# Strided attention in half-array blocks of three classes, with one exponential a pair

## The chip, the cores and the metric

The kernel runs on one core of one Trainium2 chip. A core has TensorE (PE; its weight loads are listed as PEld), VectorE (DVE), ScalarE (ACT), GpSimd (POOL) and SyncE (SP), which run side by side and wait for each other by semaphores. SP issues most transfers here, POOL the indirect ones. The metric is the time of one execution on the device, in microseconds (us); lower is better. Of the kernel before, nine runs are known: a median of 743.74 us, 740.93 to 749.4.

## The reference, cut to what matters

```python
# q, k, v: 8 batches, 8 heads, 576 positions, 64 wide, float32
rel = pos[:, None] - pos[None, :]
mask_local = (rel >= 0) & (rel < 32)                                  # heads 0 to 3
mask_strided = (rel >= 0) & (pos[None, :] % 32 == pos[:, None] % 32)  # heads 4 to 7
attn = softmax(where(mask, q @ k.T / 8, -1e9)); x = attn @ v          # then (8, 576, 512)
# a mixture of 8 experts over the 4608 rows of x
logits = x @ w_gate; local_gate = sigmoid(x @ w_local)
# row by row: the expert is argmax(logits) where local_gate < 0.5 (and at s == 0), else that of the row before
out[b, s] = softmax(logits[b, s])[e] * (relu(x[b, s] @ w1[e]) @ w2[e])
```

In the strided heads a position sees only those of its own class, pos % 32. There are 32 classes of 18 positions each, so the useful part of a 576 by 576 score matrix is 32 triangles of 18 by 18.

## The kernel before, in words

The program has two parts in one order written out by hand: `attention`, which also computes the gate logits and starts the routing, and `Experts.run`, the expert matmuls. The change lies in the first, except for the shape of one small array.

Attention goes over 32 pairs of heads, `order` = 8 batches times `PAIRS` = 4; in each batch pairs 0 and 1 are local, pairs 2 and 3 strided. A pair has two units, `g` = 0 and 1. The loop at line 414 runs over steps `n`; step `n` works on several pairs at once:

- `load(n + 4)`: q and k of the pair four ahead, by SP into one of five buffers `qk`; with the first local and the first strided pair of a batch also v (`vl`, `vs`). At `n` = 6 the weights of the first expert, 4 MB, follow in the same queue.
- `scores(n)` and `mask(n)`. Line 252 multiplies k by q in blocks. Head `h` of the pair lies on partitions 64h to 64h+63, so two heads use the upper and lower half of the array's rows. Each head has a PSUM bank of its own in the tile `sps` (two buffers). Line 256 takes the exponential on ACT into `e`. A local unit has three blocks of 96 queries by 128 keys for each head, masked afterwards by DVE (line 263). Strided units first have their mask put into PSUM by a bfloat16 matmul with the identity (line 246); no DVE mask follows.
- `store_x(n - 2)`: every second pair, the normalised rows go to DRAM (`xd`), by SP: two transfers for the local half of a batch, ten for the strided half (line 307).
- `turn_x(n - 2)`: line 317 transposes the rows of the pair into `tps`, the tile of the pool `psT`, which has one buffer; ACT copies it into `xT` (line 321).
- `values(n - 1)` and `norm(n - 1)`: line 276 multiplies `e` by v into `vps` (two buffers), in halves of 64 queries that go to the upper and the lower partitions; v has a column of ones, which gives the sums. DVE takes the reciprocal (289) and multiplies (290).
- `logits` of the batch whose last pair was turned in this step (`n - 2`, so `n` = 4b + 5): line 336, again into `psT`, then four copies into `lT`, in turn by ACT (339), DVE (340), ACT (342) and DVE (344), each waiting for the one before. `gates` a step later (`n - 3`): line 354 and some twelve small DVE instructions.
- From `n` = 19 on, for the first four batches, the router's steps: `turn`, `scan`, `hot`, `count`, `slot`, `back` (on PE, ACT, DVE), then 20 scatters on POOL (line 577), two placed in each step, and among them the gather of the first two tiles of rows for the experts (line 737) at `n` = 29.

The strided classes are in five groups: four of `GC` = 7 classes (126 positions) and one of 4 (72). A block of scores is 126 keys by 126 queries, with the classes interleaved, `position * 7 + class`. Unit 0 has groups 0 and 1 of both heads, unit 1 groups 2, 3 and 4. The mask, one bfloat16 tile `maskS`, is worked out at the start by POOL iotas and some 24 DVE instructions (lines 192 to 215), because the class of a row is a remainder by 7 or 4. In DVE's queue these stand before the first mask of the local pairs.

SP's transfers use eight completion semaphores in turn, so a transfer is issued only after the transfer eight places before it has landed.

Of the kernel before, what the change touches and what calls it, by code (L numbers as in the profile page):

```python
# [37 lines left out]
PL, GC, GT = S // STRIDE, 7, 5  # L38
GR = STRIDE - GC * (GT - 1)
GK, GL = PL * GC, PL * GR  # L40
# [102 lines left out]
def attention(ctx, tc, qkl, qks, vl, vs, wg, xd, ident, router, moe):  # L143
# [15 lines left out]
    def load(b, pair):  # L159
        local = pair < PAIRS // 2  # L160
        src = qkl if local else qks
        t = inp.tile([P, qkl.shape[-1]], F32, name="qk")
        st["qk", b, pair] = t
        nc.sync.dma_start(out=t[:, 0:src.shape[-1]], in_=src[b, pair % 2])
        if pair % 2 == 0:
            shape = [LK, LT, 4, V1] if local else [GK, GT, 4, V1]
            t = vals.tile(shape, F32, name="vl" if local else "vs")
            nc.sync.dma_start(out=t, in_=(vl if local else vs)[b])
            st["v", b, local] = t
# [22 lines left out]
    maskS = consts.tile([GK, 2 * GK + GL], BF16, name="maskS")  # L192
    for n, c in ((GK, GC), (GL, GR)):
        i = consts.tile([GK, n], I32, name=f"i{n}")
        cls = consts.tile([GK, n], F32, name=f"cls{n}")
        div = consts.tile([GK, n], F32, name=f"div{n}")
        both = []
        for mult, pattern in ((1, [[0, n]]), (0, [[1, n]])):

            nc.gpsimd.iota(i, pattern=pattern, base=0, channel_multiplier=mult)  # L200
            t = consts.tile([GK, n], F32, name=f"cls{n}{mult}")
            nc.vector.tensor_copy(t, i)
            nc.vector.tensor_scalar(i, i, 65536 // c + 1, None, Alu.mult)
            nc.vector.tensor_scalar(i, i, 16, None, Alu.arith_shift_right)
            nc.vector.tensor_copy(div, i)
            nc.vector.scalar_tensor_tensor(t, div, -float(c), t, Alu.mult, Alu.add)
            both.append(t)
        nc.vector.tensor_tensor(cls, both[0], both[1], op=Alu.not_equal)
        nc.vector.tensor_scalar(cls, cls, NEG, None, Alu.mult)
        nc.gpsimd.affine_select(out=cls, in_=cls, compare_op=Alu.is_ge, fill=NEG, base=0, pattern=[[1, n]],  # L210
                                channel_multiplier=-1)
        if n == GK:
            nc.vector.tensor_copy(maskS[:, 0:2 * n].rearrange("p (a x) -> p a x", a=2), across(cls, [n, 2, n]))
        else:
            nc.vector.tensor_copy(maskS[:, 2 * GK:], cls)
# [16 lines left out]
    def spans(u):  # L232

        if u.local:
            return [(3 * u.g + i, LQ, i * LQ) for i in range(3)]
        return [(j, GK if j < GT - 1 else GL, i * GK) for i, j in enumerate(range(2 * u.g, 2 + 3 * u.g))]

    def scores(u):
        t = st["qk", u.b, u.pair]
        kb, width = (LK, LQ) if u.local else (GK, GK)  # L240
        ps = psS.tile([P, 2, 512], F32, name="sps")
        sp = spans(u)
        n = sp[-1][2] + sp[-1][1]
        if not u.local:
            for h in range(2):
                nc.tensor.matmul(ps[0:GK, h, 0:n], lhsT=identb[0:GK, 0:GK],  # L246
                                 rhs=maskS[:, 0:n], start=True, stop=False, skip_group_check=True)
        for j, w, c in sp:
            m = kb if u.local else w
            for h in range(2):  # L250
                r = slice(h * DH, (h + 1) * DH)
                nc.tensor.matmul(ps[0:m, h, c:c + w], lhsT=t[r, S + j * width:S + j * width + m],  # L252
                                 rhs=t[r, j * width:j * width + w],
                                 start=(u.local and c == 0), stop=True, skip_group_check=True)
        e = work.tile([P, 2, 2 * GK + GL], F32, name="e")
        nc.scalar.activation(e[0:kb, :, 0:n], ps[0:kb, :, 0:n], Act.Exp, bias=0.0, scale=1.0 / DH ** 0.5)  # L256
# [9 lines left out]
    def values(u):  # L266

        vt = st["v", u.b, u.local]
        i2 = u.pair % 2
        ps = psV.tile([P, 2, 3, V1], F32, name="vps")  # L270
        for i, (j, w, c) in enumerate(spans(u)):
            m = LK if u.local else w
            for h in range(2):
                for a in range(2):
                    q0 = c + a * (w - HALF)
                    nc.tensor.matmul(ps[a * HALF:(a + 1) * HALF, h, i], lhsT=u.e[0:m, h, q0:q0 + HALF],  # L276
                                     rhs=vt[0:m, j, 2 * i2 + h], start=(i == 0 and h == 0), stop=True,
                                     skip_group_check=True)
        u.ps = ps

    def norm(u):
        i2 = u.pair % 2
        if i2 == 0 and u.g == 0:
            st["x", u.b, u.local] = rows.tile([P, LT if u.local else GT, D // 2], F32, name="xl" if u.local else "xs")
        xt = st["x", u.b, u.local]
        sp = spans(u)
        j0, n = sp[0][0], len(sp)
        rc = sums[:, u.n, :, 0:n]
        nc.vector.reciprocal(out=rc, in_=u.ps[:, :, 0:n, DH])
        nc.vector.tensor_tensor(xt[:, j0:j0 + n, i2 * P:(i2 + 1) * P].rearrange("p i (h d) -> p h i d", h=2),  # L290
                                u.ps[:, :, 0:n, 0:DH], spread(rc, [P, 2, n, DH]), op=Alu.mult)

    def store_x(u):
# [3 lines left out]
        for a in range(2):  # L297
# [5 lines left out]
            for j in range(GT):  # L303
                c = GC if j < GT - 1 else GR
                w = c * PL // 2
                o = dst.rearrange("(p c) d -> p c d", c=STRIDE)[a * PL // 2:(a + 1) * PL // 2, j * GC:j * GC + c]
                nc.sync.dma_start(out=o, in_=src[a * (P - w):a * (P - w) + w, j])

    def turn_x(b, pair):
# [5 lines left out]
        n = LT if local else GT  # L315
        for t in range(n):
            nc.tensor.transpose(ps[:, t], src[:, t], ident)  # L317
        o = st["xT", b][:, pair]

        def halves(o, i, w):  # L320
            nc.scalar.copy(out=o.rearrange("p (t a x) -> p t a x", a=2, x=w // 2),
                           in_=pick_halves(i, w))

        if local:
            halves(o, ps[:, 0:LT], LQ)
        else:
            halves(o[:, 0:4 * GK], ps[:, 0:GT - 1], GK)
            halves(o[:, 4 * GK:], ps[:, GT - 1:GT], GL)

    def logits(b):  # L330
        xT = st["xT", b]
        ps = psT.tile([P, 2, 512], F32, name="tps")
        n = GK * (GT - 1)
        for a, c in ((0, slice(0, n)), (1, slice(n, S))):
            for kk in range(DK):
# [4 lines left out]
        nc.vector.tensor_copy(lT[0:64, n:], ps[0:64, 1, 0:GL])  # L340
        o = lT[64:].rearrange("p (y c) -> p y c", c=STRIDE)
        nc.scalar.copy(out=o[:, :, 0:GC * (GT - 1)].rearrange("p y (j c) -> p j y c", c=GC),
                       in_=ps[64:, 0, 0:n].rearrange("p (j y c) -> p j y c", j=GT - 1, c=GC))
        nc.vector.tensor_copy(o[:, :, GC * (GT - 1):], ps[64:, 1, 0:GL].rearrange("p (y c) -> p y c", c=GR))
        st["lT", b] = lT

    def gates(b):

        ps = psV.tile([P, 2, 3, V1], F32, name="vps").rearrange("p a i e -> p (a i e)")
# [43 lines left out]
    for n, u in enumerate(u for both in units for u in both):  # L393
        u.n = n

    also = {n: [] for n in range(len(units) + 3)}
    also[2] = [router.constants]
    n = PAIRS * RB + 3
# [15 lines left out]
    for n in range(len(units) + 3):  # L414
# [10 lines left out]
        if 0 <= n - 2 < len(units) and n != len(units):  # L425
            turn_x(*order[n - 2])
# [6 lines left out]
        elif n == len(units) + 1:  # L433
            moe.turn(moe.first, spare, 0)
# [1034 lines left out]
```

## Time and profile before

The profiled execution took 745.11 us, 1.4 more than the median, and its span, from the first to the last instruction, is 743.3 us.

| | us |
|---|---|
| median of nine runs | 743.74 |
| profiled execution, its span | 745.11, 743.3 |
| PE busy, PEld busy | 693.7, 620.2 |
| DVE, ACT, POOL busy | 380.7, 198.9, 134.2 |
| attention part, up to the first expert matmul | 0 to 196.6 |
| one batch of attention, steps 4 to 7 | 24.33 to 43.08 |
| scatters of the router | 123 to 139, 170 to 180 |
| mean granted clock | 0.961 |

The page gives busy time by engine, then the span in 40 slices of 18.6 us, where a digit is the busy share in tenths. The timeline shows merged instructions: start in us, length in us, engine, line, operation, `out<-in`, shapes, the count, and in brackets the engine's idle time before it and what ended it. A length there reaches to the modelled end of the last matmul, which overlaps with what follows, so stretches of TensorE are best measured from start to start. A shape `64*126 64x126` is 64 rows by 126 columns of the array, and the 126 moving columns. A float32 matmul call appears as two records, each with a weight load of its own.

### The profile page before, as it was taken

To read this page: it belongs to the slowest core of one execution; us is meant where nothing else is said; L and a number is where in the kernel's file an instruction comes from. 1 tells how busy PE (TensorE), PEld (TensorE's weight loads), DVE (VectorE), ACT (ScalarE), POOL (GpSimd) and SP (SyncE) were. 2 spreads that over 40 slices of the span, in tenths; PEclk is the share of its full clock that TensorE was granted. 3 is DMA by queue.
4 is the path that set the end of the run, shared out by engine and by line. 5 is a ranking of instruction groups with operands and counts; after the bars stand their busy time and mean duration, and the time that the engine had idled before them with its cause. 6 is when DMAs were issued, how large, how long until landed. Compare 5 with 4: busy or idle time off the path is not lost.

```text
span 743.3 us, 15189 instructions
## 1 busy us (share of the span) xinstructions
PE 693.7 (93%) x6170; PEld 620.2 (83%) x6170; DVE 380.7 (51%) x896; ACT 198.9 (27%) x360; POOL 134.2 (18%) x150
## 2 busy tenths in 40 slices
PE   7999998597798799999999999999999999999993
PEld 5887887385697689899998899999999999889992
DVE  6567765372474534473563266466346646324341
ACT  2544442241321122222222222212222222212320
POOL 3000002305147221211121120131012112111001
PEclk9999999596899799999999999999999999999998
DMA  9798788732430023504322612520161342010100
GB/s 324 272 367 260 275 280 263 214 89 70 147 143 30 10 80 123 194 30 170 109 74 88 211 58 91 197 86 31 43 232 58 132 151 73 32 36 31 30 29 27
DMA packets 38057, 95.83 MB, mean 129 GB/s; under 512 B 5358, under 2 KB 14574, under 8 KB 37888
## 3 DMA queue, kind: packets, MB, share of 16 engines
q1 hardware_dynamic: 29616, 73.77, 29.1%
q0 software_dynamic: 7744, 20.08, 8.5%
q8 instruction: 64, 1.05, 0.6%
q14 instruction: 105, 0.86, 0.4%
q10 hardware_dynamic: 528, 0.07, 0.1%
HBM read 74.93 MB, written 20.02 MB: 128 GB/s over the span
## 4 chain that ended last, share of the span: by engine, by line
PE 88%; DVE 3%; issue 3%; another core or an unknown queue 2%; DMA 1%; ACT 1%; POOL 1%; POOLq 0%; DVEq 0%
PE lps L807 32%; PE mps L843 31%; PE sps L252 6%; PE vps L276 6%; PE tps L317 3%; PE xps L750 2%; PE lps L898 2%; PE mps L909 2%; PE sps L246 2%; PE vps L354 1%; PE tps L336 1%; DMA qk<-in_qks_dram 1%; DMA x<-xd,gi 1%; DVE xl L290 1%
## 5 line engine op out<-in xcount | busy, mean ns | idle before, releaser
L807 PE MATMUL lps<-tt,ws 128*128 128x128 f32 x912 | 108.8, 275 | 1.9 <-issue 1.8
L807 PEld LDWEIGHTS lps<-tt,ws 128*128 128x128 f32 x912 | 105.3, 192 | 2.2 <-issue 2.2
L763 POOL DMA_INDIRECT out_dram<-y,tab x40 | 45.8, 1146 | 332.8 <-DVE y L795 274.2
L843 PE MATMUL mps<-wt,k 128*128 128x256 f32 x456 | 101.6, 379 | 0.0
L843 PEld LDWEIGHTS mps<-wt,k 128*128 128x128 f32 x456 | 86.6, 190 | 11.8
L795 DVE TENSOR_TENSOR h<-lps,u 128x512 f32<-128x512 f32 x57 | 39.4, 691 | 80.7 <-PE lps L807 68.1
L807 PE MATMUL lps<-xt,w1t 128*128 128x128 f32 x608 | 76.0, 279 | 0.0
L807 PEld LDWEIGHTS lps<-xt,w1t 128*128 128x128 f32 x608 | 74.2, 196 | 1.9 <-issue 1.0
L843 PE MATMUL mps<-w2t,h 128*128 128x256 f32 x304 | 72.7, 382 | 0.0
L577 POOL DMA_INDIRECT slots<-tok,idx x40 | 41.0, 1024 | 145.2 <-DVE tok L568 133.2
L843 PEld LDWEIGHTS mps<-w2t,h 128*128 128x128 f32 x304 | 57.0, 193 | 7.1
L252 PE MATMUL sps<-qk 64*128 64x96 f32 (+2 forms) x704 | 54.8, 285 | 5.8 <-issue 4.6
L737 POOL DMA_INDIRECT x<-xd,gi x40 | 39.5, 986 | 112.8 <-PE lps L807 33.2
L794 ACT ACTIVATE h<-h 128x512 f32<-128x512 f32 x57 | 35.9, 630 | 88.6 <-DVE h L795 85.4
L252 PEld LDWEIGHTS sps<-qk 64*128 64x128 f32 (+2 forms) x704 | 45.1, 186 | 15.8 <-issue 13.3
L256 ACT ACTIVATE e<-sps 128x576 f32<-128x576 f32 (+1 forms) x64 | 41.4, 651 | 57.7 <-PE sps L252 39.8
L807 PE MATMUL lps<-xt,ws 128*128 128x128 f32 x304 | 39.0, 284 | 6.1 <-DVE h L795 6.1
L807 PEld LDWEIGHTS lps<-xt,ws 128*128 128x128 f32 x304 | 37.1, 199 | 6.3 <-DVE h L795 6.3
L795 DVE TENSOR_TENSOR u<-lps,p 128x512 f32<-128x512 f32 x19 | 13.1, 692 | 55.7 <-PE lps L807 51.8
L794 ACT ACTIVATE h<-lps 128x512 f32<-128x512 f32 x23 | 13.7, 597 | 97.8 <-PE lps L807 71.5
L807 PE MATMUL lps<-tt,w1t 128*128 128x128 f32 x304 | 37.9, 276 | 1.5 <-issue 1.1
L807 PEld LDWEIGHTS lps<-tt,w1t 128*128 128x128 f32 x304 | 35.8, 192 | 2.1 <-issue 1.6
(214 smaller groups left out, 915.3 us busy)
## 6 DMA issues: line engine op xcount, KB each, us to landing
w1t<-in_w_dram SPq DMA_DIRECT2D x8, 2048.0 KB
w2t<-in_w_dram SPq DMA_DIRECT2D x8, 2048.0 KB
qk<-in_qkl_dram SPq DMA_DIRECT2D x16, 592.0 KB
qk<-in_qks_dram SPq DMA_DIRECT2D x16, 576.0 KB
vl<-in_vf_dram SPq DMA_DIRECT2D x8, 780.0 KB
vs<-in_vg_dram SPq DMA_DIRECT2D x8, 639.8 KB
xd<-xl SPq DMA_DIRECT2D x16, 288.0 KB
xd<-xs SPq DMA_DIRECT2D x64, 63.0 KB
```

The source lines that it names most:

```text
L246: nc.tensor.matmul(ps[0:GK, h, 0:n], lhsT=identb[0:GK, 0:GK], rhs=maskS[:, 0:n], start=True, stop=False, skip_group_check=True)
L252: nc.tensor.matmul(ps[0:m, h, c:c + w], lhsT=t[r, S + j * width:S + j * width + m], rhs=t[r, j * width:j * width + w], start=(u.local and ...
L256: nc.scalar.activation(e[0:kb, :, 0:n], ps[0:kb, :, 0:n], Act.Exp, bias=0.0, scale=1.0 / DH ** 0.5)
L276: nc.tensor.matmul(ps[a * HALF:(a + 1) * HALF, h, i], lhsT=u.e[0:m, h, q0:q0 + HALF], rhs=vt[0:m, j, 2 * i2 + h], start=(i == 0 and h == 0 ...
L317: nc.tensor.transpose(ps[:, t], src[:, t], ident)
L577: s = self.nc.gpsimd.indirect_dma_start(out=self.T, out_offset=bass.IndirectOffsetOnAxis(ap=self.idx[0:m, t, b:b + 1], axis=0), in_=self.t ...
L737: self.nc.gpsimd.indirect_dma_start(out=r.x[:, i], out_offset=None, in_=self.xd[0:r.rows], in_offset=bass.IndirectOffsetOnAxis(ap=r.gi[i], ...
L763: s = self.nc.gpsimd.indirect_dma_start(out=self.out, out_offset=bass.IndirectOffsetOnAxis(ap=r.si[i], axis=0), in_=y[:, i], in_offset=Non ...
L794: relu = lambda o, i: nc.scalar.activation(o, i, Act.Relu)
L795: add = lambda o, i, p: nc.vector.tensor_tensor(o, p, i, op=Alu.add)
L807: nc.tensor.matmul(ps[:, f], lhsT=m[:, kk, f * P:(f + 1) * P], rhs=v[:, kk], start=(start and f == 0 and kk == 0), stop=(kk == 1), skip_gr ...
L843: nc.tensor.matmul(ps[:, 0:256], lhsT=m[:, f], rhs=v[:, f], start=(start and f == 0), stop=(f == 3), skip_group_check=True)
```

## The change: what it does

The strided pairs are cut another way; the local ones are computed as before.

- A group now has three classes, 54 positions, the classes one after another (`class * 18 + position`). The 32 classes are split in two halves of 16, 288 positions each; each half has five groups of 54 and one class of 18 left over (`GT` = 6). Half 0 lies on the upper partitions 0 to 63, half 1 on the lower.
- A score block is 54 by 54, and there are 24 calls a pair instead of 10: head `h` picks the half of the array's rows, class half `a` the half of its columns. So four blocks stand in four quarters of the array. All scores of a pair fit in 288 columns of two banks, so there are two mask calls instead of four, and one exponential of 2 x 288 columns instead of one of 2 x 252 and one of 2 x 324. Unit 1 takes over unit 0's `e`.
- The values of a unit are those of one head: 12 calls, each with 54 rows on one half of the rows and 64 columns on the same half of the columns, 24 a pair instead of 20.
- The rows of a strided pair are six tiles, not five: six transposes instead of five, a normalisation of 384 elements for each unit (before, 256 and 384). The v array of a batch grows from 126 x 1300 to 128 x 1560 elements (639.8 to 780 KB).
- The strided half of a batch is stored with eight transfers (18 partitions each) instead of ten (63 or 36 partitions each).
- The mask is made of a POOL memset, two POOL selections and four DVE copies.
- `turn_x` takes pair `n - 3` instead of `n - 2`; logits and gates follow a step later (`n` = 4b + 6 and 4b + 7), and the router's steps start at `n` = 20 instead of 19. At the end (`n` = 32 and 33) the order is caught up, with one more turn in step 32.
- In `logits`, the copies into `lT` write the positions back with another stride.

Lines of the changed kernel differ from those of the one before by one or two, or a little more.

```diff
-PL, GC, GT = S // STRIDE, 7, 5
+PL, GC, GT = S // STRIDE, 3, 6
+GW = PL * GC
+GS = S // 2
...
+    maskS = consts.tile([P, GS], BF16, name="maskS")
+    m = consts.tile([P, 2, GC, PL], F32, name="m")
+    nc.gpsimd.memset(m, 0.0)
+    nc.gpsimd.affine_select(out=m, in_=m, compare_op=Alu.is_ge, fill=NEG, base=0,
+                            pattern=[[-HALF, 2], [-PL, GC], [0, PL]], channel_multiplier=1)
+    nc.gpsimd.affine_select(out=m, in_=m, compare_op=Alu.is_ge, fill=NEG, base=0,
+                            pattern=[[HALF, 2], [PL, GC], [1, PL]], channel_multiplier=-1)
+    for a in range(2):
+        r = slice(a * HALF, (a + 1) * HALF)
+        src = m[r, a].rearrange("p c x -> p (c x)")
+        nc.vector.tensor_copy(maskS[r, 0:(GT - 1) * GW].rearrange("p (j x) -> p j x", j=GT - 1),
+                              across(src, [HALF, GT - 1, GW]))
+        nc.vector.tensor_copy(maskS[r, (GT - 1) * GW:], src[:, 0:PL])
...
     def scores(u):
         t = st["qk", u.b, u.pair]
+        if not u.local and u.g:
+            u.e = u.other.e
+            return
         ps = psS.tile([P, 2, 512], F32, name="sps")
+        if u.local:
+            n = 3 * LQ
+            spans = [(j * LQ, (j - 3 * u.g) * LQ, LQ, LK, (0,)) for j in range(3 * u.g, 3 * u.g + 3)]
+        else:
+            n = GS
             for h in range(2):
+                nc.tensor.matmul(ps[:, h, 0:n], lhsT=identb, rhs=maskS, start=True, stop=False, skip_group_check=True)
+            spans = [(j * GW, j * GW, w, w, (0, GS)) for j, w in enumerate([GW] * (GT - 1) + [PL])]
+        for q, c, w, m, parts in spans:
             for h in range(2):
                 r = slice(h * DH, (h + 1) * DH)
+                for a, k in enumerate(parts):
+                    q0 = q if u.local else q + k
+                    nc.tensor.matmul(ps[a * HALF:a * HALF + m, h, c:c + w], lhsT=t[r, S + q + k:S + q + k + m],
+                                     rhs=t[r, q0:q0 + w], start=(u.local and c == 0), stop=True, skip_group_check=True)
+        e = work.tile([P, 2, GS], F32, name="e")
+        nc.scalar.activation(e[:, :, 0:n], ps[:, :, 0:n], Act.Exp, bias=0.0, scale=1.0 / DH ** 0.5)
...
     def values(u):
...
+            for j in range(GT):
                 for a in range(2):
+                    q0 = min(j * GW, GS - HALF)
+                    r = slice(a * HALF, a * HALF + GW)
+                    nc.tensor.matmul(ps[a * HALF:(a + 1) * HALF, j], lhsT=u.e[r, u.g, q0:q0 + HALF],
+                                     rhs=vt[r, j, 2 * i2 + u.g], start=(j == 0), stop=True, skip_group_check=True)
...
     def store_x(u):
...
+            for c in range(GC):
+                p = a * HALF + c * PL
+                nc.sync.dma_start(out=o[:, c:last:GC], in_=src[p:p + PL, 0:GT - 1])
+            p = (a + 1) * HALF - PL
+            nc.sync.dma_start(out=o[:, last:], in_=src[p:p + PL, GT - 1:])
...
-    n = PAIRS * RB + 3
+    n = PAIRS * RB + 4
...
-        if 0 <= n - 2 < len(units) and n != len(units):
-            turn_x(*order[n - 2])
+        if 0 <= n - 3 < len(units) and n <= len(units):
+            turn_x(*order[n - 3])
...
         elif n == len(units) + 1:
+            turn_x(*order[n - 2])
             moe.turn(moe.first, spare, 0)
...
-        for d, do in ((3, gates), (2, logits)):
+        late = n < len(units)
+        for d, do in ((3 + late, gates), (2 + late, logits)):
```

## The prediction

> **What bounds the kernel now.** I read the page's busy row and its slices first, then a table of stages, then the timeline of one batch, then the start and the DMA queue. "Code call" is one matmul call in the source; a float32 call stands in the trace as two records.
>
> ```profile
> PE 693.7 (93%) x6170; PEld 620.2 (83%) x6170; DVE 380.7 (51%) x896; ACT 198.9 (27%) x360; POOL 134.2 (18%) x150
> ...
> PE   7999998597798799999999999999999999999993
> ```
>
> TensorE bounds the whole; the dips are in the first eleven slices, the attention part, which ends at 196.6 us. Only that part changes. In the table of stages (length; busy time of each engine; clock, DMA share, GB/s) three stretches are full of TensorE work and two are not:
>
> ```profile
> 12.40:64.50 52.10, 51.54 (x887) 43.16 (x889) 33.28 (x109) 23.60 (x43) 1.29 (x3) 0.97 0.88 320
> ...
> 71.30:127.00 55.70, 53.83 (x907) 44.99 (x907) 37.72 (x115) 25.83 (x48) 3.00 (x3) 1.00 0.79 272
> 127.00:143.00 16.00, 5.93 (x61) 4.75 (x59) 2.83 (x10) 1.79 (x4) 8.66 (x9) 0.55 0.82 232
> ...
> 170.00:182.00 12.00, 7.45 (x37) 4.97 (x36) 1.61 (x5) 0.00 (x0) 7.73 (x8) 0.62 0.22 54
> ```
>
> 127 to 143 and 170 to 182 are where POOL issues the router's scatters and every other engine stands, put down to "issue" and "remote"; the scatters stay. So in the full stretches a microsecond of TensorE work is a microsecond, unless something is late next. One batch (18.75 us: steps start at 24.33, 43.08 and 61.83), from the timeline:
>
> ```profile
> 82.81 0.77 PE L317 MATMUL tps<-ident,xs 128*128 128x128 f32 x5
> ...
> 83.50 1.39 PE L276 MATMUL vps<-vs,e 126*64 126x65 f32 x40
> ...
> 84.82 1.58 PE L252 MATMUL sps<-qk 64*128 64x96 f32 x24
> ...
> 87.03 1.62 PE L276 MATMUL vps<-vl,e 128*64 128x65 f32 x48
> ...
> 88.58 1.18 PE L336 MATMUL tps<-xT,wgs 128*32 128x504 f32 x16
> ...
> 89.69 0.43 PE L246 MATMUL sps<-maskS,identb 126*126 126x252 bf16 x2
> ...
> 90.05 0.71 PE L252 MATMUL sps<-qk 64*126 64x126 f32 x8
> ...
> 90.68 0.49 PE L246 MATMUL sps<-maskS,identb 126*126 126x324 bf16 x2
> ...
> 91.10 0.83 PE L252 MATMUL sps<-qk 64*126 64x126 f32 x12
> ...
> 91.32 0.24 DVE L344 COPY lT<-tps 64x72 f32<-64x72 f32 x1 [0.67 <-ACT lT L342]
> ...
> 91.86 0.88 PE L317 MATMUL tps<-ident,xl 128*128 128x128 f32 x6
> ```
>
> From start to start: scores of a strided pair take 0.36+0.63+0.42+0.76 = 2.17 us (89.69 to 91.86); its values 1.32 (83.50 to 84.82); a local pair's values 1.55; turning five tiles 0.69, six 0.81 (91.86 to 92.67). Forty value records against 48 make a record 29 ns, a pair 58, where the expert matmuls pay 114 ns for 128 columns and 216 for 256 (chain rows: 12.76 us for 56, 10.36 for 48), so 0.8 ns a column and 12 fixed, 64 for 65 columns alone. Hence the two column halves run together.
>
> **The change, part by part**, per strided pair (16 of them), against this execution's own 745.1 us.
>
> *Scores.* Four mask calls become two of 288 columns: 0.39 between the 0.36 and 0.42 above, instead of 0.78. Ten score calls (20 records) become 24 (48 records) of 54 columns or fewer, in four quarters. No row shows four quarters with both rows and columns halved. L336 puts four column groups of 504 columns together (16 records in 1.1 us; at 0.8 a column and 12 ns each they would take 3.9 alone), so four streams do run at once. Best end: twelve groups of four, ten of them 54/65 of 58 = 50 ns, two narrow ones 30, plus the 0.19 that a block pays on entry (0.63 less four pairs of 112) = 0.75, against 1.39. Worst end: one after the other, 48 x 55 + 0.19 = 2.8. I take the best, being nearest to L336: scores 1.14 instead of 2.17, **-1.03 x 16 = -16.5**; the worst end is +16.5 on the same term.
>
> *Values.* 20 calls become 24, each on a diagonal quarter: 48 records, 1.55 like a local pair, **+0.23 x 16 = +3.7**. If the diagonal quarters do not overlap, +1.4 more a pair (24 x 58).
>
> *Turns.* Six tiles instead of five: **+0.12 x 16 = +1.9**. Turning a step later adds no instruction. It moves six transposes and their ACT copies, behind them the logits (TensorE, ACT, DVE), the gates, and the router's steps with POOL's scatters and gathers, past one step's scores, values and norms; SP's stores keep their step, so no load is passed. The turn now waits for norms long finished, and the turn left over is paid in step 32.
>
> *What is late next.* Logits stay in the step of their last turn, but that is now the step of the first strided pair (n = 4b+6), so what follows them is another strided scores block, as before, only shorter. Line 317's transposes need the one `psT` buffer that the four `lT` copies empty, ACT and DVE in turn; the last, L344, ends at 91.56, 1.87 us after the scores began. Today 2.17 covers it. With 1.14 it does not: TensorE waits 0.75, **x 7 = +5.3**; behind it stand values, norms and gates of that step. If the scores get only half their gain, the wait is 0.25, so this returns part of any miss. Below nothing it cannot be, as the copies stay.
>
> *Start.* The old mask is built by some 24 DVE instructions before the first L263:
>
> ```profile
> 8.54 1.58 PE L252 MATMUL sps<-qk 64*128 64x96 f32 x24 [0.44 <-DMA qk<-in_qkl_dram]
> ...
> 11.57 2.76 DVE L263 TENSOR_TENSOR e<-e,maskL 128x576 f32<-128x576 f32 x4
> ...
> 12.37 2.85 PE L276 MATMUL vps<-vl,e 128*64 128x65 f32 x48 [2.25 <-DVE e L263]
> ...
> 15.15 0.68 PE L246 MATMUL sps<-maskS,identb 126*126 126x252 bf16 x2
> ```
>
> The new one is three POOL instructions and four DVE copies after maskL (ready at 3.5), under 2 us by the 0.2 to 0.3 of each today. Then L263 follows exp at 8.2, values follow scores at 10.1, and the first strided scores start near 11.7 instead of 15.15: **-3.4**. Part of it is that the clock, 0.5 from 12.43 to 15.84, need not fall. Ends: 0 (loads late instead) and -3.4.
>
> *Loads and stores.* Steps 2 and 3 need q and k of the strided pairs; 2.5 MB are queued up to the first, 3.9 up to the second, and the table of stages has 290 GB/s for 0 to 12.4 us, so about 9 and 13 us: in time (the second is wanted near 14.5). Later SP is the narrow place: the chain shows
>
> ```profile
> 64.50 6.74 DMA qk<-in_qks_dram
> 71.29 0.71 PE sps L252 x8
> ```
>
> though without it step 14 would start at 70.6 (one batch after 51.83), so it costs 0.7. SP issued that load late, after ten strided stores at 0.79 us each. Eight stores save 1.6 us a batch; the larger v load (640 to 780 KB) takes back 0.4. I work out SP's side: first stores 5.5 us earlier, bounded by the landing of the load ahead of them at 30 us, so the load for step 14 is issued near 58 and lands near 64.8; TensorE would want it at 63.5. **Wait 1.3 instead of 0.7: +0.6.** Ends: -0.7, and +8 if the transfers do not move up at all.
>
> *Costed at nothing.* One exponential of 576 (652 ns, the local row) for 504 and 648 (591 and 712): ACT is 45% busy there and nothing waits for it. Norms of 384 elements for 256: +0.13 us of DVE a pair, under the values; if uncovered, 2.1 in all. The router's gather comes a step later, needed at 190.3 and issued by 170 now; if uncovered, a step, 4 us.
>
> Sum: -16.5 +3.7 +1.9 +5.3 -3.4 +0.6 = -8.4, so 736.7 for the profiled execution. That one ran 1.4 over the median 743.74, hence **735.3** as median.
>
> **Rivals.**
> *B, records cannot follow each other so fast.* The densest long stretch in the trace is 29 ns a record. Held to it, 48 records take 1.39+0.19: +0.83 a pair, 13.3, and the 5.3 of waiting goes; net +8.0, 743. For: no row is denser for long. Against: L336's groups of four. The Trainium skill, "TensorE: Matmul & The Clock Gate", Back-to-back issue gap, has a floor of about 25 ns from start to start; if it binds across quarters too, an estimate from that page is 741. No run here shows the floor itself.
>
> *C, the other side: the values' quarters do not overlap.* Both row halves write one bank (`vps`), at different partitions. Price 1.4 x 16 = +22, less 1.3 for the load wait, which goes: 756. It decides from 8.4/(16 x 24) = 22 ns more a pair of records. Against: L276 today writes one bank from two column halves together, but from the same rows. The Trainium skill, "TensorEngine Tiling (Array Packing)", Gotcha 1, says that different row tiles cannot use one PSUM bank at the same time; by it C holds and 756 follows, by the L276 row A holds. I keep to the row.
>
> *D, the stalls at the scatters grow.* The two stretches leave TensorE 14.6 us idle and at half clock, some 24 lost in all (15.8 and 8.4 over the usual batch). The strided pair now has 208 TensorE records and weight loads instead of 138, a batch 784 instead of 644, a fifth more to be issued. If the loss grows by that fifth, +5: 740; if the second burst now also holds up the tail behind step 32, up to 751.
>
> **How the numbers follow.** A (quarters overlap, the wait for `lT` appears) 0.56, own range 731 to 740; B 0.16, 740 to 746; C 0.13, 751 to 760; D 0.15, 736 to 751. A measurement here tells 0.5% from nothing, so faster is below 740.0 and slower above 747.5. Faster: 0.93 of A, a fifth of B, a quarter of D = 0.59. Slower: nearly all of C, a fifth of B, 0.4 of D = 0.22. The rest, 0.19, is the same. The range 730 to 751 leaves out C and little else, under 0.2.
>
> **What would show it.** Right: strided scores about 1.1 us from the first mask to the turn or to the end of work, values of strided pairs 1.5 to 1.6, a gap of 0.7 before the transposes of every second strided step put down to the DVE copy of `lT`, first strided scores near 12 us, the batch about 17.9 us. Wrong: 48 score records taking over 1.2 us (B), 48 value records over 2.5 us (C), load waits of several us near 60, or stretches of "issue" and "remote" longer than 28 us together (D).

## The result, and the profile after

The changed kernel took 750.04 us (median of 18 runs, 747.53 to 757.42), against 742.37 us for the kernel before over all its runs beside it. The ratio is 1.0107, 95% interval 1.0086 to 1.0129: 1.1% slower, where 735.3 us and a gain of 1% were forecast. The time lies in the forecast's range, but on the other side of no change. The profiled execution took 753.25 us, its span is 751.5 us, against 745.11 and 743.3 before.

Two rows of the page after: busy time by engine, and the 40 slices (18.8 us each) with the granted clock.

```profile
PE 691.2 (92%) x6730; PEld 621.3 (83%) x6730; DVE 379.0 (50%) x874; ACT 192.7 (26%) x344; POOL 134.3 (18%) x147
...
PE   8889998497699699999999999999999999999993
...
PEclk9999999789589799999999999999999999999997
```

TensorE has 560 records more and 2.5 us less busy time; it is the time between them that grew. The stages after (length; busy time of PE, PEld, DVE, ACT, POOL; granted clock, DMA share, GB/s):

```profile
12.40:64.50 52.10, 45.64 (x1036) 38.67 (x1027) 32.05 (x105) 20.54 (x36) 0.00 (x0) 0.97 0.96 356
71.30:127.00 55.70, 48.28 (x1002) 41.13 (x1002) 35.49 (x107) 22.52 (x41) 0.00 (x0) 0.93 0.80 272
137.00:153.00 16.00, 6.80 (x70) 5.09 (x72) 2.40 (x10) 1.28 (x3) 8.42 (x9) 0.59 0.35 97
180.00:196.00 16.00, 8.42 (x114) 7.13 (x110) 3.37 (x16) 1.31 (x3) 10.78 (x12) 0.63 0.18 44
```

In the two full stretches TensorE was busy 51.54 and 53.83 us before; now it is 45.64 and 48.28 of the same lengths. "A microsecond of TensorE work is a microsecond" no longer holds there. The timeline of TensorE shows where (start, length, line, shapes, records, and the idle time before with its releaser):

```profile
85.46 1.62 PE L275 MATMUL vps<-vs,e 54*64 54x65 f32 x48
87.01 1.58 PE L243 MATMUL sps<-qk 64*128 64x96 f32 x24
...
90.88 0.42 PE L235 MATMUL sps<-maskS,identb 128*128 128x288 bf16 x2
91.23 0.89 PE L243 MATMUL sps<-qk 64*54 64x54 f32 x48
92.04 0.88 PE L319 MATMUL tps<-ident,xs 128*128 128x128 f32 x6
92.85 1.62 PE L267 MATMUL vps<-vl,e 128*64 128x65 f32 x48
94.40 1.18 PE L335 MATMUL tps<-xT,wgs 128*32 128x504 f32 x16
95.51 0.42 PE L235 MATMUL sps<-maskS,identb 128*128 128x288 bf16 x2
95.86 0.89 PE L243 MATMUL sps<-qk 64*54 64x54 f32 x48
97.97 0.84 PE L319 MATMUL tps<-ident,xl 128*128 128x128 f32 x6 [1.23 <-DVE lT L342]
98.74 1.62 PE L275 MATMUL vps<-vs,e 54*64 54x65 f32 x48
100.81 1.25 PE L352 MATMUL vps<-fold,lT 128*128 128x9 f32 x12 [0.45 <-DVE sums L285]
101.99 2.70 PE L243 MATMUL sps<-qk 64*128 64x96 f32 x24
104.62 1.35 PE L319 MATMUL tps<-ident,xl 128*128 128x128 f32 x6
```

The scores of a strided pair are as short as forecast: from 90.88 to the turn at 92.04 is 1.16 us, of which the 48 records in four quarters take 0.81 (91.23 to 92.04), 17 ns each. The 48 value records of a strided pair take 1.55 (85.46 to 87.01), like those of a local one (92.85 to 94.40). Then TensorE waits 1.23 us for `lT`, 0.45 at the gates, and in this execution runs the next step at half clock (scores 2.70 where 1.58 is the rule). The copies that it waits for, on ACT:

```profile
95.64 0.57 ACT L338 COPY lT<-tps 64x504 f32<-64x504 f32 x1 [1.99 <-PE tps L335]
96.50 1.00 ACT L341 COPY lT<-tps 64x504 f32<-64x504 f32 x1 [0.29 <-DVE lT L339]
```

The second takes 1.00 us; the line that it replaces took 0.607 on average in the profile of before (count; busy, mean ns):

```profile
L342 ACT COPY lT<-tps 64x504 f32<-64x504 f32 x8 | 4.9, 607 | 3.1 <-DVE lT L340 3.1
```

The start went as forecast, with an idle time "issue" that it did not have before:

```profile
11.77 0.42 PE L235 MATMUL sps<-maskS,identb 128*128 128x288 bf16 x2
...
16.78 0.78 PE L243 MATMUL sps<-qk 64*54 64x54 f32 x37 [1.55 <-issue]
```

Read by the start of a step, the kernel after is ahead by 4.5 us at step 4 (19.8 against 24.3), by 1.9 at step 12 (59.9 against 61.8), then behind by 2.2 at step 24, by 3.2 at step 31 and by 10.9 at the first expert matmul (207.4 against 196.5); the experts give 2.7 back. The lead of the start is lost batch by batch, and the tail loses more.

### The profile page after: what moved, and what is told of

Read it like the earlier page. It is cut to its first block, busy times and chain, and to the rows that moved or that the text cites. A ratio compares the mean times of both kernels' runs of the same rounds, so it can differ in the third digit from the quotient of the medians.

```text
span 751.5 us, 16240 instructions
## 1 busy us (share of the span) xinstructions
PE 691.2 (92%) x6730; PEld 621.3 (83%) x6730; DVE 379.0 (50%) x874; ACT 192.7 (26%) x344; POOL 134.3 (18%) x147
## 4 chain that ended last, share of the span: by engine, by line
PE 83%; DMA 7%; issue 3%; another core or an unknown queue 3%; DVE 2%; ACT 1%; SPq 0%; POOL 0%; DVEq 0%; POOLq 0%
PE lps L809 32%; PE mps L845 30%; PE sps L243 4%; PE tps L319 3%; PE vps L267 2%; PE vps L275 2%; PE xps L752 2%; DMA xd<-xl 2%; PE lps L900 2%; PE mps L911 2%; DMA qk<-in_qkl_dram 2%; PE vps L352 1%; DMA qk<-in_qks_dram 1%; DMA xd<-xs 1%
## 5 line engine op out<-in xcount | busy, mean ns | idle before, releaser
L845 PEld LDWEIGHTS mps<-wt,k 128*128 128x128 f32 x456 | 86.5, 190 | 13.2 <-issue 1.5
L243 PE MATMUL sps<-qk 64*54 64x54 f32 (+2 forms) x1152 | 45.9, 240 | 10.9 <-issue 10.8
L243 PEld LDWEIGHTS sps<-qk 64*54 64x54 f32 (+2 forms) x1152 | 39.1, 150 | 18.2 <-issue 16.2
L246 ACT ACTIVATE e<-sps 128x576 f32<-128x576 f32 x48 | 31.2, 650 | 62.8 <-PE sps L243 62.0
L796 ACT ACTIVATE h<-lps 128x512 f32<-128x512 f32 x23 | 13.7, 597 | 96.0 <-PE lps L809 73.8
L285 DVE RECIPROCAL sums<-vps 128x6 f32<-128x6 f32 x64 | 12.3, 192 | 50.2 <-remote 21.2
```

Of the source, the lines that this page charges most:

```text
L243: nc.tensor.matmul(ps[a * HALF:a * HALF + m, h, c:c + w], lhsT=t[r, S + q + k:S + q + k + m], rhs=t[r, q0:q0 + w], start=(u.local and c == ...
L246: nc.scalar.activation(e[:, :, 0:n], ps[:, :, 0:n], Act.Exp, bias=0.0, scale=1.0 / DH ** 0.5)
L796: relu = lambda o, i: nc.scalar.activation(o, i, Act.Relu)
L845: nc.tensor.matmul(ps[:, 0:256], lhsT=m[:, f], rhs=v[:, f], start=(start and f == 0), stop=(f == 3), skip_group_check=True)
```

## The experiments

They ran on other chips than the first one, on which the kernel before takes 709.5 to 711.1 us; each ratio is against the kernel before in the same call. There the first stretch at the scatters hardly exists (step 25 takes 4.9 us instead of 20.7), so what these chips show is the rest of the loss. The last two columns split the mean span of the runs that the ratio uses: the time lost to half clock, span times (1 - mean granted clock), and what is left, the span reckoned at full clock. Time in which TensorE idles at half clock counts as lost too. The standard error is 0.6 to 1.9 us for the clock column and 0.3 to 0.8 for the last, but 3.8 and 1.1 for "before, more records", which has three runs. From call to call the kernel before gives 708.0 to 709.4, 10.7 to 12.4 and 696.8 to 697.3; the table has its last call.

| kernel | ratio, 95% interval | span | lost to clock | at full clock |
|---|---|---|---|---|
| before (17 to 25 runs a call) | 1 | 708.9 | 11.7 | 697.3 |
| after | 1.0083 (1.0034 to 1.0131); 1.0110 (1.0073 to 1.0148) | 714.0; 716.9 | 15.4; 17.3 | 698.6; 699.6 |
| after, logits in the scores' buffer | 1.0001 (0.9967 to 1.0034); 1.0003 (0.9970 to 1.0036) | 709.5; 708.9 | 16.7; 17.0 | 692.8; 691.9 |
| after, turn not shifted | 0.9988 (0.9953 to 1.0022); 1.0007 (0.9972 to 1.0043) | 708.5; 709.4 | 13.0; 13.0 | 695.5; 696.5 |
| after, runs in `lT` | 1.0027 (0.9989 to 1.0066) | 711.0 | 15.2 | 695.9 |
| scores' buffer and runs | 0.9982 (0.9941 to 1.0023) | 707.9 | 16.7 | 691.2 |
| scores' buffer and runs, 6 large score matmuls a strided pair | 0.9957 (0.9930 to 0.9985) | 705.9 | 15.2 | 690.6 |
| not shifted and runs | 0.9974 (0.9930 to 1.0018) | 707.1 | 13.5 | 693.6 |
| all three | 0.9937 (0.9887 to 0.9987) | 704.2 | 13.6 | 690.6 |
| all three, slot counts elsewhere too | 0.9920 (0.9884 to 0.9957) | 702.3 | 10.1 | 692.1 |
| before, longer copy | 1.0133 (1.0067 to 1.0198) | 718.4 | 12.4 | 706.0 |
| before, more records | 1.0142 (1.0063 to 1.0221) | 720.2 | 13.2 | 706.9 |
| before, turn shifted | 1.0112 (1.0071 to 1.0152) | 716.0 | 17.7 | 698.4 |

**Logits in another buffer.** Theory W says the loss is the wait for `lT` and the half clock seen behind it; theory T, that the shift of the turn and what hangs on it costs the time.

```diff
-        ps = psT.tile([P, 2, 512], F32, name="tps")
+        ps = psS.tile([P, 2, 512], F32, name="sps")
         n = PL * (512 // PL)
```

> The kernel after, with the logits in one of the two buffers of the scores and not in the single buffer of the turns, so that the next turn no longer waits for the four copies to lT. Theory W (the loss is TensorE's wait for those copies, 1.2 us in each of seven batches, and the half clock that follows it for 3.4 us in the step after): 750.0 - 7 x 1.22 - about 4 x 1.5 = 735.5 us (733 to 739), L319 shows no wait of 1.2 us for lT, and the half clock at 61, 82, 102 and 126 us is gone. Theory T (the loss is in the stretch of the scatters and in the router's later finish, whatever the wait): 745 to 750 us, with the half clock left where it was or the gain given back at the scatters.

1.0001, between the two. The wait is gone, and the span at full clock is 6 to 8 us shorter than that of after, close to the 8.5 us of the waits. But the clock loses as much as in after, and part of the wait comes back at the gates, which need `lT` too and now queue behind DVE.

**The wait put into the kernel before.**

```diff
         nc.scalar.copy(out=o[:, :, 0:GC * (GT - 1)].rearrange("p y (j c) -> p j y c", c=GC),
                        in_=ps[64:, 0, 0:n].rearrange("p (j y c) -> p j y c", j=GT - 1, c=GC))
+        nc.scalar.copy(out=o[:, :, 0:GC * (GT - 1)].rearrange("p y (j c) -> p j y c", c=GC),
+                       in_=ps[64:, 0, 0:n].rearrange("p (j y c) -> p j y c", j=GT - 1, c=GC))
+        nc.scalar.copy(out=o[:, :, 0:GC * (GT - 1)].rearrange("p y (j c) -> p j y c", c=GC),
+                       in_=ps[64:, 0, 0:n].rearrange("p (j y c) -> p j y c", j=GT - 1, c=GC))
```

> The kernel before, with the ACT copy to lT at L342 issued three times (0.607 us each), so that the chain behind the logits ends 1.21 us later: 1.87 + 1.21 = 3.08 us after the scores begin, against 2.17 us of strided scores. Theory W: TensorE then waits about 0.9 us at the first transpose in seven batches, and falls to half clock once a batch as in the kernel after: 742.4 + 7 x 0.9 + about 4 x 1.5 = 755 us (750 to 757). Theory W without the clock (the wait costs its own length and no more): 747 to 750. Theory T: 742 to 744.

+9.1 us: 8.2 us of waiting at L317 in seven batches, the view of waits says, and 1.3 more at one of the gates. The clock loses 0.3 us more than before in the same call, within the error of 1.3. So the wait costs its own length, and the half clock of some 6 us that theory W adds does not come in this kernel; that half of the theory falls.

**Runs in `lT`.**

```diff
-        o = lT[64:].rearrange("p (y c) -> p c y", c=STRIDE)
-        nc.scalar.copy(out=o[:, 0:n // PL], in_=ps[64:, 0, 0:n].rearrange("p (c y) -> p c y", y=PL))
-        nc.vector.tensor_copy(o[:, n // PL:], ps[64:, 1, 0:S - n].rearrange("p (c y) -> p c y", y=PL))
+        o = lT[64:].rearrange("p (y c) -> p y c", c=STRIDE)
+        nc.scalar.copy(out=o[:, :, 0:n // PL], in_=ps[64:, 0, 0:n].rearrange("p (c y) -> p y c", y=PL))
+        nc.vector.tensor_copy(o[:, :, n // PL:], ps[64:, 1, 0:S - n].rearrange("p (c y) -> p y c", y=PL))
```

> The kernel after, with the two strided copies to lT going through the classes of one position in a row: writes in runs of 28 and 4 elements, reads strided, where it wrote single elements 128 bytes apart and read runs of 18. If the strided write made L341 1.00 instead of 0.61 us: L341 takes about 0.6 us, TensorE's wait falls from 1.22 to about 0.8 us: 750 - 7 x 0.4 = 747 us, and 741 us (739 to 744) if a wait of 0.8 us also leaves the clock alone. If the strided read costs as much: 750 us and L341 about 1.0.

The groups of ACT between 15 and 130 us (line, shapes, count; busy, mean ns; idle before):

```profile
L341 ACT COPY lT<-tps 64x504 f32<-64x504 f32 x5 | 2.9, 574 | 1.5 <-DVE lT L339 1.5
```

574 ns instead of 997. It is the write in single elements 128 bytes apart that costs 0.42 us, not a strided read, which this variant has instead. The wait falls to 0.8 us, the time to 1.003, and the span at full clock by 2.7 to 3.7 us, where 7 x 0.4 = 2.8 follow.

**The turn not shifted.**

```diff
-        if 0 <= n - 3 < len(units) and n <= len(units):
-            turn_x(*order[n - 3])
+        if 0 <= n - 2 < len(units) and n != len(units):
+            turn_x(*order[n - 2])
...
-        late = n < len(units)
+        late = 0
```

and the router from `n` = 19 again.

> The kernel after, with turn, logits, gates and router at the steps they have in the kernel before. Theory W: the wait for lT stays, since the step that follows the logits is a strided one again (1.14 us of scores), and the turn now also waits for the norm of the step just before it, which strided scores of 1.14 us cover no longer: 750 to 758 us. Theory T (the shift is what cost the time): 740 to 746 us.

0.9988, as theory T had it. TensorE still waits 9.3 us for `lT` in all (8.5 in after; between 8 and 200 us: sum, times, longest),

```profile
PE tps L319 <- DVE lT L342: 9.3, 7, 1.7
```

and yet this gives back as much as taking the wait away. Two parts of the change each return nearly the whole loss.

**Both kernels on the chips of the experiments.**

> The kernel after, unchanged, beside the kernel before on the chip of this call. The chip of the first four experiments ran the kernel before in 711.0 us instead of 742.4, and the experiments there stood at 1.000 (logits in the scores' buffer), 1.013 (before with the longer copy), 1.003 (runs in lT) and 0.999 (turn not shifted) of it, so the kernel after has to be seen on such a chip too. If what it loses is the wait of 1.2 us: 1.011 times the time of before, whatever the chip, as in the result. If it loses by something that the first chip alone has (its stretch of the scatters, 17 us at half clock, or its clock): 1.000 to 1.004 on a fast chip.

1.0083: the loss is nearly the same where the first chip's stretch of the scatters is missing. The kernel before beside it gives the trace to compare with.

> The kernel before, unchanged, for its trace on the chip of this call: step starts, the stretch of the scatters, the clock. Its time is that of before, 711 or 742 us by the chip. On a fast chip its stretch from the first gather to the experts' first product should be 15 to 20 us shorter than in the profile of before.

711.23 us; its first strided scores start at 15.2 and its step 4 at 26.8 us, with half clock from 11.3 to 21.5. The first expert matmul starts at 172.4 us, 24 earlier than on the first chip. TensorE's waits between 8 and 200 us, in after (sum, times, longest):

```profile
PE tps L319 <- DVE lT L342: 8.5, 7, 1.2
PE vps L352 <- DVE sums L285: 2.9, 6, 0.8
PE tps L335 <- issue: 2.1, 2, 1.5
PE sps L243 <- issue: 1.8, 2, 1.6
PE vps L352 <- DVE lT L342: 1.7, 1, 1.7
...
PE tps L319 <- issue: 0.4, 1, 0.4
PE vps L275 <- issue: 0.3, 1, 0.3
```

and in before:

```profile
PE vps L276 <- DVE e L263: 2.1, 1, 2.1
PE vps L354 <- DVE sums L289: 2.0, 6, 0.6
PE vps L354 <- DVE lT L344: 1.3, 1, 1.3
PE sps L252 <- DMA qk<-in_qkl_dram: 1.1, 1, 1.1
...
PE tps L317 <- DVE lT L344: 0.2, 1, 0.2
...
PE vps L276 <- issue: 0.2, 1, 0.2
```

So there are 8.5 us for `lT` and, new to me, 4.6 us with no releaser, in six places. The DMA records of the trace say what these are: the instruction queue moves 16 KB at a time, and each of the six ends 1.2 to 1.6 us after such a packet has landed (in the variant with the scores' buffer, seven of seven; with all three edits, six of six). All but one in each of the first two, and all in the third, lie before 107 us; in after the DMA engines are 0.87 to 1.00 busy with loads from 10 to 100 us. Call it theory F: TensorE runs out of instructions.

**Two edits at once.**

> Logits in the scores' buffer and runs in lT together: neither the wait for lT nor, at the gates, more than the 0.3 to 0.5 us for DVE's reciprocal (the first experiment waited 3.7 us at the gates in five batches, up to 2.1 at once, since DVE's second copy follows ACT's slow one). Theory W: 0.995 to 0.999 of before, the lowest of the variants with the shifted turn. If the time of the attention is covered by what comes behind it, 1.000 as the first experiment.

> The turn not shifted, with runs in lT: the turn and the router as early as in before, and the wait for lT of 1.3 us on average (6.7 in five) shortened by 0.4. 7 x 0.4 = 2.8 us below the variant with the turn alone put back (0.999 of before): 0.995. If the waits for lT cost nothing beyond 0.8 us since something else is late then: 0.999.

0.9982 and 0.9974: neither is told apart from before. In the first, no wait for `lT` is left at the turn, and still it stands 7 us above the forecast's 0.989; 16.7 us go to the clock, and 6.7 us to waits with no releaser.

**Fewer, larger instructions.** On the variant of the scores' buffer and runs:

```diff
+        if not u.local:
+            for i in range(6):
+                k = (0, P, GS - P)[i // 2]
+                nc.tensor.matmul(ps[:, i % 2, k:k + P], lhsT=t[:, S + k:S + k + P], rhs=t[:, k:k + P], start=False,
+                                 stop=True, skip_group_check=True)
+            spans = []
```

> The variant with logits in the scores' buffer and runs in lT, in which the 24 quarter matmuls of a strided pair's scores are replaced by 6 of 128 x 128 x 128 on the same tile: about as long on TensorE (six transposes of that size take 0.81 us, the 24 took 0.81), a quarter of the instructions; it doesn't compute the strided scores. Theory F (TensorE runs out of instructions: each of its waits with no releaser in the kernel after and in this variant ends 1.2 to 1.5 us after a packet of 16 KB on the instruction queue has landed): those waits, 6.5 us in the variant's profile between 8 and 200 us, fall below 1.5 us, and its time from 0.998 to 0.991 of before; to 0.985 if the windows of half clock behind these waits (at 40 and 136 us) go with them. If the waits have another cause: they stay near 6 us, and the time at 0.998.

Not one wait without a releaser of 0.1 us or more is left between 8 and 200 us, where the variant had 6.7 us of them; theory F's sign. The time is 0.9957 (0.9930 to 0.9985), not 0.991: the six matmuls take 1.33 us (87.84 to 89.18) instead of 0.81,

```profile
87.84 1.50 PE L241 MATMUL sps<-qk 128*128 128x128 f32 x12
89.18 0.82 PE L325 MATMUL tps<-ident,xl 128*128 128x128 f32 x6
```

so 16 x 0.52 = 8.3 us of work were added, and the span at full clock is nevertheless no longer (690.6 against 691.2). How much of this is owed to the smaller count and how much to the added time, in which instructions can arrive, this run does not separate.

**More instructions in the kernel before.**

```diff
+        for i in range(0 if u.local else 8):
+            a, h = i % 2, i // 2 % 2
+            r = slice(h * DH, (h + 1) * DH)
+            nc.tensor.matmul(ps[a * HALF:(a + 1) * HALF, h, 400:402], lhsT=t[r, S:S + HALF], rhs=t[r, 0:2],
+                             start=False, stop=True, skip_group_check=True)
```

> The kernel before, with 8 more matmuls of 2 columns for each strided unit, written to columns of the PSUM tile that nobody reads: 55 instead of 39 matmuls a strided pair, as many as the kernel after has (56), with no other wait changed. Their own length by the 17 to 29 ns of a record: 16 records a unit, 32 units, 9 to 15 us. Theory F: waits with no releaser, next to none in the kernel before between 8 and 130 us on such a chip, appear as in the kernel after, 3 us or more: +12 to +20 us, 1.017 to 1.028 of before. If the fetch keeps up at this density as long as nothing else is shorter: the waits stay below 1 us and the time is 1.012 to 1.021.

Each block of 16 added records takes 0.34 us (21 ns each), 10.9 us for 32; at full clock the span grew by 9.6.

```profile
99.40 0.41 PE L258 MATMUL sps<-qk 64*64 64x2 f32 x16
99.74 0.49 PE L246 MATMUL sps<-maskS,identb 126*126 126x324 bf16 x2
```

The only wait without a releaser in the view is this:

```profile
PE vps L281 <- issue: 0.2, 1, 0.2
```

So the number of instructions alone does not starve TensorE: the kernel before with as many records as after, in batches of 20.1 us or more, is fed in time. After is not, although its batches take 19.2 to 20.4 us with their waits on such a chip, nor is the variant with the scores' buffer and runs (18.5 us at the shortest). What besides the number decides, the spacing of the records within a batch for one, is not shown.

**All three, and the slot counts.**

> All three at once: logits in the scores' buffer, runs in lT, turn and router not shifted. The variant with runs and no shift has 5.9 us of waits for lT left, and 1.9 us of waits with no releaser. If each of these waits costs its length: 0.997 - 0.008 = 0.989 of before. Theory F says that TensorE, freed of the waits for lT in which the instruction queue caught up, then waits for instructions instead, 3 us or more: 0.993 to 0.996.

0.9937 (0.9887 to 0.9987), 704.73 us against 710.89: faster than both kernels. 3.2 us of waits without a releaser remain, as theory F had it, and half clock from 111.0 to 124.6 us, behind the router's waits.

```diff
         def slot():
-            ps = bank()
+            ps = (other or bank)()
```

where `other` gives a buffer of the scores.

> All three parts of the variant before, and the router's slot counts in one of the scores' buffers too, so that the turn behind them does not wait for DVE's total. In the variant's profile TensorE idles 0.58 + 0.76 (gates, behind DVE's scan of 1.35 us) + 1.17 us (total) between 104.9 and 111.6 us, and runs at half clock from 111.0 to 124.6. If it is this accumulation of idle time that halves the clock: with 1.17 us gone the half clock there is gone too or shorter, and the time falls by 1.2 + 0 to 6.8 us: 697 to 703 us against 704.7, 0.981 to 0.992 of before. If the half clock comes without regard to this wait: 703.5 us, 0.992.

0.9920 (0.9884 to 0.9957). In its trace the wait for `total` is gone and the half clock there is 3.4 us instead of 13.7. Over its runs the clock loses 3.5 us less, but the kernel before beside it also lost 1.7 less (10.7 against 12.4), and the remaining 1.8 us are within the error. Nor is the time as a whole told apart from that of the variant before it.

**The shift alone, and the main comparisons in one call.**

```diff
-        if 0 <= n - 2 < len(units) and n != len(units):
-            turn_x(*order[n - 2])
+        if 0 <= n - 3 < len(units) and n <= len(units):
+            turn_x(*order[n - 3])
...
-        for d, do in ((3, gates), (2, logits)):
+        late = n < len(units)
+        for d, do in ((3 + late, gates), (2 + late, logits)):
```

in the kernel before, with the left-over turn in step 32 and the router from `n` = 20.

> The kernel before with turn, logits, gates and router one step later, and nothing else. If the shift costs by itself (the router and the gather end later, and what follows waits): 1.005 to 1.010 of before. If it costs only together with the short scores (TensorE catches up with the instruction queue and idles for it): 0.998 to 1.003, with no wait without a releaser between 8 and 130 us.

> The kernel after, unchanged, for the comparison with the next two on the same chip: 1.006 to 1.011 of before.

> The kernel after with the turn not shifted, again, in the call of the kernel after: 0.997 to 1.001 of before if the first result holds, 0.008 below the kernel after; 1.003 to 1.006 if it was the spread of the measurement, and the wait for lT, left as it was, is the larger part.

> The kernel after with the logits in the scores' buffer, again, in the call of the kernel after: 0.998 to 1.002 of before if the first result holds. The traces price the wait at 7 x 1.2 = 8.5 us = 0.012; if the rest is taken by waits for DVE at the gates (3.7 in place of 2.4 us), by waits without a releaser and by half clock, these rows show it again.

The shift alone, with the old scores, makes the kernel before slower by 1.12% (0.71 to 1.52%), as much as the whole change; beside it after stands at 1.0110, without the shift at 1.0007, with the logits elsewhere at 1.0003. There is no wait without a releaser, and none for `lT` at the turn. What there is, in its one trace: a lead of 4.9 us at step 4 (21.9 against 26.8) that is down to 0.2 at step 16, after two waits for loads (2.9 us) and a window of half clock, and more half clock later.

```profile
70.72 0.71 PE L252 MATMUL sps<-qk 64*126 64x126 f32 x8 [1.88 <-DMA qk<-in_qks_dram]
...
72.98 1.33 PE L317 MATMUL tps<-ident,xs 128*128 128x128 f32 x5
```

TensorE waits 1.88 us for q and k of step 14, and runs the next 3.4 us at half clock (a turn of five tiles takes 1.33 instead of 0.77). The stage table has, for the shift alone:

```profile
120.00:137.00 17.00, 15.80 (x175) 14.45 (x175) 10.52 (x36) 4.18 (x8) 3.86 (x4) 0.60 0.89 292
```

and for the kernel before on such a chip:

```profile
120.00:137.00 17.00, 16.52 (x292) 13.67 (x290) 12.20 (x44) 8.42 (x15) 9.16 (x9) 1.00 0.83 214
```

In the same 17 us, with TensorE as busy, 175 records instead of 292 are done, at a clock of 0.60. Over all runs the shift costs 6.0 us of clock (standard error 1.9) and 1.1 us besides. The table says the same throughout: the rows with the shift, whatever else they change, lose 15.2 to 17.7 us to the clock, those without it 10.1 to 13.6.

## Why the prediction was wrong

By its own steps, with the traces of both kernels on one chip of the second kind (after's profile there: span 714.1 against 709.5):

- *Scores*, -1.03 a pair: right. 1.16 instead of 2.18 us, -16.3 in all. Rival B, that records cannot follow each other faster than 29 ns, is refuted at 17 ns. The Trainium skill, "TensorE: Matmul & The Clock Gate", Part 1 ("Wait — 56ns, not 53.3ns?"), has a floor of about 25 ns from start to start; across four quarters the trace shows less.
- *Values*, +3.7, and *turns*, +1.9: right, 1.55 and 0.81 us. Rival C is refuted: the diagonal quarters write one PSUM bank, and their records follow each other in 32 ns, as a local pair's do. The Trainium skill, "TensorEngine Tiling (Array Packing)", Gotcha 1, says that different row tiles cannot use one PSUM bank at the same time; for these blocks the trace does not bear it out.
- *Start*, -3.4: right. The first strided scores start at 11.77 instead of 15.15. Step 4 starts 4.5 us earlier on the first chip, which takes in what two shorter strided blocks give and a wait of 1.55 costs; on the second kind 6.9 earlier, since the half clock of before, 11.3 to 21.5, does not come.
- *Loads and stores*, +0.6: it did not come. Between 8 and 200 us neither trace of after has a wait of TensorE for q or k.
- *What is late next*, +5.3: the mechanism was right, the size was off. It took L341 for as long as the line it replaces, 0.607 us; the strided write makes it 1.00, and TensorE waits 1.22, x 7 = 8.5. The diff had shown the new stride.
- *Turning a step later adds no instruction*, priced at nothing, with the router's later gather "needed at 190.3 and issued by 170 now": this is the step that failed. Alone it costs 1.1%, and without it the rest of the change is worth 0.9988 and 1.0007 of before. It was costed by what it adds to queues, and nothing was charged for what TensorE's lead runs into or for the clock. What the runs showed in its place: 6.0 us of clock and 1.1 besides in the kernel before; in the changed kernel 7.5 us (716.9 against 709.4), 4.3 of them clock and 3.1 at full clock, where TensorE waits 4.6 and 6.5 us without a releaser with the shift and 1.4 and 2.2 without it.
- The extra instructions were weighed once, in rival D, and only at the scatters. There the first stretch did not grow on the first chip (step 26 takes 18.2 us, step 25 before 20.7), but the stretch from step 31 to the experts did, 30.8 us against 23.1, so what D says of the "tail behind step 32" fits; whether the count or the later router stretched it is not shown, as no experiment ran on that chip. Elsewhere they cost what no term had: 4.6 us of waiting for instructions.

The sum on the second kind, from the two traces, up to the first expert matmul: scores -16.3, values +3.7, turns +1.8; gone from the start, the wait for the mask, one for a load and 10.2 us of half clock (1.1 of it idle, so 4.6 lost), -2.1 - 1.1 - 4.6 = -7.8; for `lT` +8.3, at the gates +1.0, without a releaser +4.4; half clock at 119.4 to 122.8 and 139.9 to 150.1, half of 13.6 = +6.8. Together +1.9; measured +4.0 (176.4 against 172.4). Some 2 us have no place, and these two executions lie closer together (4.6 us in span) than the means of the two kernels (5.6 and 8.0).

On the first chip the two traces point the same way. TensorE works at half clock for 49.2 us of after (77.9 us of such windows less 28.7 in which it idles) and for 34.2 of before (60.6 less 26.4); half of the difference is 7.5 us, of 8.2 by which the spans differ. That it is the shift there too is not shown.

That it is the half clock which the shift brings, 17.7 us lost against 11.7, is measured; why it does is not settled. The half-clock windows last 3.4 us or a multiple. Most came behind windows in which TensorE had idled 0.7 to 1.9 us of the 3.4, but 15 of the 56 falls before 205 us came behind windows with 0.5 us or less, and 1.65 us in the kernel before with the longer copy brought none. So the idle time of the window ahead does not decide by itself. The Trainium skill, "TensorE: Matmul & The Clock Gate", Part 1 ("What's actually happening"), has the clock fall after an idle window of about 3.4 us; the windows just before the falls at 72.0 (shift alone) and 102.2 us (after, first chip) were idle for 1.9 and 0.5 us, and the clock fell.

## What to carry to other kernels

Where an engine is nearly full, a step that is only moved is not free: price what its lead runs into (loads, copies, the fetch of instructions), and compare the clock of the two orders over many runs, as one trace says little of it. If a block is shortened, list everything that its length covered, each with the duration of the new form of the instruction, strides included. Small matmuls in four quarters pay (48 records in 0.81 us for 20 in 1.39), but so many instructions in so little time can outrun the instruction queue while the DMA engines are busy.

## What the runs showed of the hardware

- Four quarters of the array take 48 records of 54 columns or fewer in 0.81 us, 17 ns from one to the next.
- An ACT copy of 64 x 504 elements took 1.00 us when it wrote single elements 128 bytes apart, 0.57 when it wrote runs and read strided.
- The instruction queue moves packets of 16 KB. All 19 waits without a releaser in after, in the variant with the scores' buffer and in that with all three edits, outside the scatters, ended 1.2 to 1.6 us after one had landed.
- The kernel before took 742 us on one chip and 709.5 to 711.1 on others. Of the 32 us, 15.8 lie in the stretch at the first scatters (20.7 against 4.9 us) and 9.0 between step 31 and the experts (23.1 against 14.1).
